# A cast behind a multiply, a scaling in two groups, keys ahead of values, and last columns of 384 and 128, in a fused attention and feed-forward kernel

## The chip, the cores and the metric

The kernel runs on one core of a Trainium2 chip. The metric is the device time of one execution in microseconds (us), as the median of several executions; lower is better. All executions quoted here were fast: TensorE's granted clock was 0.995 to 1.0 in them. Engine names are those of the profile: PE is TensorE, PEld its weight loads, DVE VectorE, ACT ScalarE, POOL GpSimd, SP SyncE; SPq and ACTq are the queues from which SP and ACT issue DMAs.

## The reference

Attention of a linear kind (8 batches, 8 heads, 576 positions, 64 wide) is followed by a gated feed-forward block, called FFN below.

```python
q_s = exp(q - max(q, -1));  q_s = q_s / (sum(q_s, -1) + 1e-9)     # over the 64 columns
k_s = exp(k - max(k, 2));   k_s = k_s / (sum(k_s, 2) + 1e-9)      # over the 576 positions
kv  = einsum('bhsd,bhse->bhde', k_s, v)
a   = einsum('bhsd,bhde->bhse', q_s, kv)                          # float32
x   = a.transpose(0, 2, 1, 3).reshape(4608, 512)
g   = x @ w_gate;  silu = g / (1 + exp(-g))                       # w_gate, w_val: 512 x 1536
out = (silu * (x @ w_val)) @ w_out                                # w_out: 1536 x 512, float32
```

## The kernel before

Heads are handled in two groups G of four heads. For a batch, ACT takes the exponentials of queries and keys, DVE normalises the queries (sum, reciprocal, multiply into `qs`), PE turns `qs`, multiplies keys with values (`kv`), DVE scales that by the key sums (`kn`), and PE multiplies the two into `xp`, which is copied into `xt`. The FFN then works through `xt` in chunks of tokens. A chunk has 12 units; unit m makes 128 of the 1536 hidden columns:

```python
def m_unit(c0, n, m, by_group=False):          # (cut)
    ...                                        # 4 matmuls g_ps <- xt,wg and 4 u_ps <- xt,wv
    nc.scalar.activation(out=sg, in_=g_ps, func=AF.Silu)
    nc.vector.tensor_mul(hr[:, m, ...], sg, u_ps)
```

PSUM is the memory that PE writes its results to. Every PSUM tile comes from one pool of eight banks, so a PE unit may have to wait until an earlier Silu has read its bank. Attention of later batches is woven between the units. Batch 1's is done between the first batch's FFN and the first chunk:

```python
def cast_v(b, G):                              # POOL: values to bf16
    return nc.gpsimd.tensor_copy(out=vbs[G][:, :, :, 0:64], in_=raw["v", b, G]...)

norm_sum(1, 0)
i = norm_mul(1, 0)
cast_v(1, 0)
c = cast_v(1, 1)                               # the second cast waits for the first multiply
tc.add_manual_dep(c.ins, i.ins.name, SYNC, reason="order of the vector port")
norm_sum(1, 1)
... # exponentials of the keys, turns of group 0, part of the output matmuls of block 2
norm_mul(1, 1)
... # turns of group 1
kv_both(1)                                     # K^T V of both groups in two banks
scale_both(1)                                  # two reciprocals and two multiplies on DVE
```

Loads are issued from SP in program order; `load_kv(b)` issues keys, values, keys, values. In the first chunk (batch 2) the exponentials of batch 3's keys stand ahead of the seventh unit:

```python
chunks = [(S, 448)] + [(c, 512) for c in range(1024, n_tok, 512)]
for ci, (c0, n) in enumerate(chunks):          # (cut: only what concerns chunk 0)
    for m in range(MT):
        if ci == 0 and m == 6:
            exp_of("k", b + 1, 0)              # ACT, needs batch 3's first keys
            exp_of("k", b + 1, 1)              # ACT, needs batch 3's second keys
            ...
        m_unit(c0, n, m)
```

The last 128 rows are made in two halves of columns, so that the first half is stored while the second is computed:

```python
def o_last(j):
    for c0 in (0, 256):
        o_ps = bank("o_ps")
        ...                                    # 12 matmuls of 256 columns
        nc.vector.tensor_copy(out=o_sb[:, c0:c0 + 256], in_=o_ps[:, 0:256])
        store(j, o_sb, c0, c0 + 256, (nc.sync, nc.scalar))   # 64 rows from each queue
```

The softmax here doesn't subtract the row's maximum and nothing guards it: scores larger than these inputs give would overflow.

## Time and profile before

| | before |
|---|---|
| time, first three runs | 314.22 us (313.61 to 314.38) |
| time, six runs, in the rounds of the result below | 313.74 us (313.46 to 314.38) |
| span in the profile | 311.3 us |
| PE busy | 301.7 us, 97% |
| first FFN matmul | 14.1 us |
| first FFN matmul of chunk 0 / of chunk 1 | 51.51 / 72.33 us |
| last matmul starts / last store lands | 306.49 / 310.12 us |

The head of the page of the kernel before gives the span, and for each engine busy time, share and number of instructions.

```profile
span 311.3 us, 5449 instructions
...
PE 301.7 (97%) x2182; PEld 149.7 (48%) x2182; DVE 161.3 (52%) x274; ACT 145.9 (47%) x214; POOL 31.2 (10%) x39
```

PE bounds the kernel. Whatever the change gains has to come from the ten microseconds in which PE is not busy, of which the head and the tail hold most. The view of waits of the kernel before, for PE (waited for, us in total, times, longest), lists two between 40 and 60 us:

```profile
PE tp L162 <- DVE qs L147: 0.6, 1, 0.6
...
PE g_ps L282 <- ACT sg L289: 0.3, 1, 0.3
```

The timeline of the kernel before shows what these are. Its columns are start, duration, engine, line, operation, tiles written and read, shapes, count, and in brackets the idle time ahead with its releaser.

```profile
44.31 1.15 POOL L122 CAST vb<-v 128x1152 bf16<-128x1152 f32 x1 [0.28 <-DVE rs L133]
44.62 2.04 DVE L147 TENSOR_TENSOR qs<-eq,rr 128x1152 bf16<-128x1152 bf16 x1
46.72 0.68 PE L162 MATMUL tp<-ident,qs 128*128 128x128 bf16 x9 [0.64 <-DVE qs L147]
...
54.91 1.16 ACT L119 ACTIVATE ek<-k 128x1152 bf16<-128x1152 f32 x1 [0.68 <-DMA k<-in_k_dram]
57.98 0.92 PE L282 MATMUL g_ps<-xt,wg 128*128 128x448 bf16 x4 [0.26 <-ACT sg L289]
...
64.66 1.16 ACT L119 ACTIVATE ek<-k 128x1152 bf16<-128x1152 f32 x1 [0.35 <-DMA k<-in_k_dram]
65.84 1.28 ACT L289 ACT_TABLE_LOAD   x1
67.90 0.92 PE L282 MATMUL g_ps<-xt,wg 128*128 128x448 bf16 x4
```

Three places matter. At 44.6 us the multiply for `qs` took 2.04 us while POOL cast values, and PE waited 0.64 us for it. At 54.9 us ACT had waited 0.68 us for batch 2's last keys; its first Silu came late and PE waited for a bank. At 64.7 us the same happened with batch 3's second keys, but there PE reached the unit concerned (unit 11, that is the eleventh, at 67.90 us) just as the bank came free, so PE lost nothing. This third place is called the gate below.

The tail, by the timeline of the kernel before: the last copy.

```profile
306.80 0.42 DVE L331 COPY o_sb<-o_ps 128x256 f32<-128x256 f32 x1 [0.89 <-PE o_ps L327]
```

And by the DMA view of the kernel before, from 307.4 us to the end (packets, MB and share of the 16 DMA engines' time in the window; then each issue with KB and us from issue to landing):

```profile
q14 instruction: 2, 0.02, 2.4%
...
out_dram<-o_sb SPq DMA_DIRECT2D x1, 64.0 KB, 2.7
out_dram<-o_sb ACTq DMA_DIRECT2D x1, 64.0 KB, 2.9
```

The last two stores of 64 KB took 2.7 and 2.9 us to land.

### The profile page before, as it was taken

What the parts mean: (1) busy time and instruction counts of PE and PEld (TensorE: products, weight loads), DVE (VectorE), ACT (ScalarE), POOL (GpSimd) and SP (SyncE); (2) the same over time, 40 slices, a digit from 0 to 9 for tenths busy, and PEclk for the clock granted to TensorE, in tenths of its full rate; (3) what the DMA queues carried; (4) which work ended last, traced back from release to release, by engine and by line L of the source; (5) the groups of instructions that cost most, each with busy time, mean ns of one, the idle gap of its engine ahead of it and who ended that gap; (6) DMA issues with size and microseconds to landing.
All of it is one profiled execution on the core that took longest, in us unless ns stands there. A gap on an engine that the chain in (4) does not pass through costs nothing.

```text
span 311.3 us, 5449 instructions
## 1 busy us (share of the span) xinstructions
PE 301.7 (97%) x2182; PEld 149.7 (48%) x2182; DVE 161.3 (52%) x274; ACT 145.9 (47%) x214; POOL 31.2 (10%) x39
## 2 busy tenths in 40 slices
PE   6899999999999999999999999999999999999994
PEld 2578745555444444454445444544444444444443
DVE  3844487945853566365826493539353324333321
ACT  5843558785674375547464737454042113212200
POOL 2960031120200110002000200000000000000000
PEclk9999999999999999999999999999999999999998
DMA  7999999899346916490739252505310211021034
GB/s 274 190 198 204 278 388 390 283 258 392 81 86 180 345 28 119 117 393 17 143 71 375 81 124 61 180 0 106 73 34 2 67 24 44 2 68 25 9 71 101
DMA packets 41690, 45.78 MB, mean 147 GB/s; under 512 B 18496, under 2 KB 25664, under 8 KB 41664
## 3 DMA queue, kind: packets, MB, share of 16 engines
q1 hardware_dynamic: 32752, 39.99, 43.3%
q0 software_dynamic: 8752, 5.31, 11.9%
q8 instruction: 17, 0.28, 0.4%
q10 hardware_dynamic: 160, 0.13, 0.2%
q14 instruction: 9, 0.07, 0.1%
HBM read 37.75 MB, written 9.44 MB: 152 GB/s over the span
## 4 chain that ended last, share of the span: by engine, by line
PE 80%; DMA 12%; POOL 4%; ACT 1%; SPq 1%; issue 0%; DVE 0%; ACTq 0%
PE o_ps L307 26%; PE g_ps L282 26%; PE u_ps L282 25%; DMA k<-in_k_dram 8%; DMA wo<-in_moe_w_out_dram 4%; POOL wg L94 1%; POOL wv L94 1%; PE kv L187 1%; PE xp L243 1%; PE o_ps L327 1%; ACT ek L119 1%; SPq L77 1%; POOL v L345 0%; ACT L289 0%; POOL v L342 0%
## 5 line engine op out<-in xcount | busy, mean ns | idle before, releaser
L289 ACT ACTIVATE sg<-g_ps 128x512 bf16<-128x512 f32 (+2 forms) x120 | 64.5, 554 | 133.0 <-PE g_ps L282 133.0
L290 DVE TENSOR_TENSOR hr<-sg,u_ps 128x512 bf16<-128x512 bf16 (+2 forms) x120 | 74.2, 630 | 87.9 <-PE u_ps L282 81.4
L282 PE MATMUL g_ps<-xt,wg 128*128 128x512 bf16 (+2 forms) x480 | 111.5, 358 | 0.3 <-ACT sg L289 0.3
L282 PE MATMUL u_ps<-xt,wv 128*128 128x512 bf16 (+2 forms) x480 | 111.4, 358 | 0.0
L307 PE MATMUL o_ps<-wo,hr 128*128 128x512 bf16 x420 | 93.9, 379 | 0.0
L282 PEld LDWEIGHTS <-wv 128*128 128x128 bf16 x480 | 46.9, 98 | 46.5
L282 PEld LDWEIGHTS <-wg 128*128 128x128 bf16 x480 | 46.2, 98 | 45.8 <-issue 0.7
L307 PEld LDWEIGHTS <-hr 128*128 128x128 bf16 x420 | 40.8, 98 | 48.6
L108 DVE COPY o_sb<-o_ps 128x512 f32<-128x512 f32 x33 | 22.4, 680 | 39.2 <-PE o_ps L307 39.2
L122 POOL CAST vb<-v 128x1152 bf16<-128x1152 f32 x14 | 16.3, 1162 | 137.2 <-DMA v<-in_v_dram 77.6
L133 DVE TENSOR_REDUCE rs<-eq 128x18 f32<-128x1152 bf16 (+2 forms) x18 | 21.7, 1214 | 12.8 <-ACT eq L119 12.8
L147 DVE TENSOR_TENSOR qs<-eq,rr 128x1152 bf16<-128x1152 bf16 (+2 forms) x18 | 22.4, 1254 | 0.1
L119 ACT ACTIVATE eq<-q 128x1152 bf16<-128x1152 f32 (+2 forms) x18 | 18.3, 1051 | 3.5 <-DMA q<-in_q_dram 3.5
L119 ACT ACTIVATE ek<-k 128x1152 bf16<-128x1152 f32 (+2 forms) x17 | 18.3, 1102 | 3.4 <-DMA k<-in_k_dram 3.3
L289 ACT ACT_TABLE_LOAD x12 | 15.4, 1283 | 0.2
L119 ACT ACT_TABLE_LOAD x11 | 14.1, 1283 | 0.2
L257 ACT CAST xt<-xp 128x512 bf16<-128x512 f32 x14 | 7.8, 586 | 4.1 <-PE xp L243 4.1
L258 DVE CAST xt<-xp 128x512 bf16<-128x512 f32 x14 | 9.0, 682 | 0.9 <-PE xp L243 0.9
L372 PE MATMUL idle<-zero 128*128 128x512 bf16 x20 | 6.5, 480 | 2.7 <-DVE rs L133 1.4
L187 PEld LDWEIGHTS <-ek 64*64 64x64 bf16 x504 | 6.4, 107 | 1.7 <-ACT ek L119 0.4
L187 PE MATMUL kv<-vb,ek 64*64 64x65 bf16 x504 | 6.8, 195 | 0.0
L243 PE MATMUL xp<-qt,kn 64*64 64x512 bf16 (+1 forms) x112 | 6.7, 292 | 0.0
(43 smaller groups left out, 63.2 us busy)
## 6 DMA issues: line engine op xcount, KB each, us to landing
q<-in_q_dram SPq DMA_DIRECT2D x16, 576.0 KB, 5.6
out_dram<-o_sb SPq DMA_DIRECT2D x70, 128.0 KB, 2.3
k<-in_k_dram SPq DMA_DIRECT2D x15, 576.0 KB, 7.9
v<-in_v_dram SPq DMA_DIRECT2D x14, 576.0 KB, 9.5
wo<-in_moe_w_out_dram POOLq DMA_DIRECT2D x4, 384.0 KB, 14.4
wg<-in_moe_w_gate_dram POOLq DMA_DIRECT2D x2, 384.0 KB, 10.1
wv<-in_moe_w_val_dram POOLq DMA_DIRECT2D x2, 384.0 KB, 11.4
wg<-in_moe_w_gate_dram POOLq DMA_DIRECT2D x2, 256.0 KB, 6.4
```

Source lines behind the costliest of these rows:

```text
L108: eng.tensor_copy(out=out, in_=in_)
L119: nc.scalar.activation(out=e[:, t0:t1], in_=src[:, t0:t1], func=AF.Exp)
L122: return nc.gpsimd.tensor_copy(out=vbs[G][:, :, :, 0:64], in_=raw["v", b, G].rearrange("p h (t d) -> p t h d", d=64),)
L133: i = nc.vector.reduce_sum(out=rs[:, 2 * t0:2 * t1], in_=eq2[:, 2 * t0:2 * t1, :], axis=mybir.AxisListType.X)
L147: last = eng.tensor_mul(qs[:, t0:t1, :].rearrange("p t (h d) -> p (t h) d", d=64), eq2[:, 2 * t0:2 * t1, :], s["rr"][:, 2 * t0:2 * t1].to_ ...
L187: nc.tensor.matmul(out=kv[g][HALF[h], c:c + 65], lhsT=ek[HALF[g], t, h, :], rhs=vbs[G][HALF[g], t, h, :], start=(t == 0), stop=(t == T - 1),)
L243: nc.tensor.matmul(out=o[h][HALF[g], c:c + 64 * (t1 - t0)], lhsT=kn[HALF[h], g, G, :], rhs=qt[G][HALF[h], t0:t1, 64 * g:64 * g + 64], star ...
L258: nc.vector.tensor_copy(out=xt[:, 2 * G + 1, c0:c0 + 512], in_=main[G][1])
L282: nc.tensor.matmul(out=gu[a][i][:, 0:w_], lhsT=(wg, wv)[a][:, kk, ms], rhs=xt[:, kk, c:c + w_], start=(kk == 0), stop=(kk == KT - 1),)
L289: nc.scalar.activation(out=sg[:, 0:w_], in_=g_ps[:, 0:w_], func=AF.Silu)
L290: nc.vector.tensor_mul(hr[:, m, r:r + w_], sg[:, 0:w_], u_ps[:, 0:w_])
L307: nc.tensor.matmul(out=o_ps, lhsT=hr[:, m, r0:r0 + 128], rhs=wo[:, m, :], start=(m == 0), stop=(m == MT - 1),)
```

## The change

The intent was to keep POOL off the vector port while the second query multiply runs, to hand K^T V of batch 1 on group by group, to have batch 2's keys loaded ahead of its values since ACT needs them first, to spread copies of the head over engines and banks, and to leave less to copy and store after the last matmul.

```diff
-        for c0 in (0, 256):
+        for c0, n in ((0, 384), (384, 128)):         # o_last; 256 becomes n in its body
...
         turn_pe(0, 1, 0)                              # head
+        turn_out(0, 1, 0, nc.vector)
+        xp0 = x_mm(0, 0, 0), x_mm(0, 0, 1)
         turn_pe(0, 1, 1)
-        turn_out(0, 1, 0, nc.vector)
         turn_out(0, 1, 1, nc.vector)
-        xp0 = x_mm(0, 0, 0), x_mm(0, 0, 1)
         kv_first(1, *BANKS[0])
         kv_first(1, *BANKS[1])
-        x_out(0, 0, 0, xp0[0])
+        x_out(0, 0, 0, xp0[0], (nc.scalar, None))
         x_out(0, 0, 1, xp0[1], (nc.scalar, None))
         scale_first(1, nc.vector)
+        x_out(0, 0, 0, xp0[0], (None, nc.scalar))
         x_out(0, 0, 1, xp0[1], (None, nc.vector))
...
-        load("q", q, 2, 0)                            # loads of batch 2
-        load("q", q, 2, 1)
-        load_kv(2)
+        for what, src in (("q", q), ("k", k), ("v", v)):
+            for G in range(NG):
+                load(what, src, 2, G)
...
-        i = norm_mul(1, 0)                            # batch 1
-        cast_v(1, 0)
-        c = cast_v(1, 1)
-        tc.add_manual_dep(c.ins, i.ins.name, SYNC, reason="order of the vector port")
+        norm_mul(1, 0)
...
-        norm_mul(1, 1)
+        i = norm_mul(1, 1)
+        cast_v(1, 0)
+        c = cast_v(1, 1)
+        tc.add_manual_dep(c.ins, i.ins.name, SYNC, reason="order of the vector port")
...
-        st["kv", 1] = [bank("kv") for _ in range(2)]
+        kv = [[bank("kv") for _ in range(2)] for _ in range(NG)]
-        kv_both(1)
-        scale_both(1)
+        kn = st["kn", 1] = at.tile([128, 2, NG, 64], BF16, tag="kn2", name="kn2")
+        for G in range(NG):
+            kv_mm(1, G, kv[G], 0)
+            for g in range(2):
+                kvr = at.tile([128, 1], FP32, tag=f"kvr{g}", name="kvr")
+                nc.vector.reciprocal(out=kvr, in_=kv[G][g][:, 64:65])
+                nc.vector.tensor_scalar_mul(kn[:, g, G], kv[G][g][:, 0:64], kvr)
```

Cut away: pieces of output matmuls are moved to fill PE (4 and 10 become 6 and 9), and `exp_of("k", 1, 0)` stands four operations later. In the built programs, DVE has 455 instructions instead of 452 (the scaling by group adds four, one copy goes to ACT).

More of the change, by code (lines that the diff above doesn't have):

```diff
@@ L217, in kv_both @@
     def kv_both(b):
-        if ("kv", b) not in st:
-            st["kv", b] = [bank("kv") for _ in range(2)]
+        kv = st["kv", b] = [bank("kv") for _ in range(2)]
         for G in range(NG):
-            kv_mm(b, G, st["kv", b], 256 * G)
+            kv_mm(b, G, kv, 256 * G)
     def scale_both(b):
@@ L327, in o_last @@
                 nc.tensor.matmul(
-                    out=o_ps[:, 0:256], lhsT=hr[:, m, r0:r0 + 128], rhs=wo[:, m, c0:c0 + 256],
+                    out=o_ps[:, 0:n], lhsT=hr[:, m, r0:r0 + 128], rhs=wo[:, m, c0:c0 + n],
                     start=(m == 0), stop=(m == MT - 1),
                 )
-            nc.vector.tensor_copy(out=o_sb[:, c0:c0 + 256], in_=o_ps[:, 0:256])
-            store(j, o_sb, c0, c0 + 256, (nc.sync, nc.scalar))
+            nc.vector.tensor_copy(out=o_sb[:, c0:c0 + n], in_=o_ps[:, 0:n])
+            store(j, o_sb, c0, c0 + n, (nc.sync, nc.scalar))
     make_identity(nc, ident)
@@ L460 @@
         o_out(1, o_mm(1), nc.scalar)
-        exp_of("k", 1, 0)
         p2 = o_mm(2, m1=4)
@@ L465 @@
         turn_out(1, 0, 0, nc.scalar)
+        exp_of("k", 1, 0)
         exp_of("k", 1, 1, BANKS)
-        norm_mul(1, 1)
+        i = norm_mul(1, 1)
+        cast_v(1, 0)
+        c = cast_v(1, 1)
+        tc.add_manual_dep(c.ins, i.ins.name, SYNC, reason="order of the vector port")
         o_mm(2, p2, m0=4)
@@ L473 @@
         turn_out(1, 1, 1, nc.vector)
-        st["kv", 1] = [bank("kv") for _ in range(2)]
-        p3 = o_mm(3, m1=4)
+        kv = [[bank("kv") for _ in range(2)] for _ in range(NG)]
+        p3 = o_mm(3, m1=6)
         o_out(2, p2)
-        kv_both(1)
-        scale_both(1)
+        kn = st["kn", 1] = at.tile([128, 2, NG, 64], BF16, tag="kn2", name="kn2")
[5 more added lines that the diff above has]
+                nc.vector.tensor_scalar_mul(kn[:, g, G], kv[G][g][:, 0:64], kvr)
         exp_of("q", 2, 0)
-        o_mm(3, p3, m0=4, m1=10)
+        o_mm(3, p3, m0=6, m1=9)
         x_and_next_kv(1, with_kv=False)
-        o_mm(3, p3, m0=10)
+        o_mm(3, p3, m0=9)
         o_out(3, p3)
```

## The prediction

> **What bounds the kernel.** The page gives PE 301.7 of 311.3 us busy (97%), and the waits of PE sum to under 5 us. Besides the head (14.1 us to the first FFN matmul) the timeline leaves:
> - 46.1 to 46.7 us: PE waits for batch 1's second normalised query group (0.64 us). That DVE multiply took 2.04 us, its twin 1.36, while the POOL value cast (44.31, 1.15 us) ran. The Trainium skill, "SBUF — State Buffer", section "SBUF: two separate sides", calls the port pair shared by Vector and GpSimd an exclusive lock held for a whole instruction; 0.68 us lost against 0.84 us of overlap agrees roughly.
> - 57.55 to 57.98 us: PE waits for a PSUM bank that the first Silu of batch 2's first chunk (57.39 us) frees, late because ACT waited 0.68 us for batch 2's last keys (they landed at 54.83) and then loaded a table (1.28 us).
> - The tail: last matmul 306.8, copy 0.42 us, last store issued 307.26, landed 310.1.
>
> **What the change does.**
> 1. Cast moved behind the multiply: it ends near 45.98, so PE resumes near 46.05: 0.65 us.
> 2. K^T V scaled by group: eight short DVE operations (start to start about 0.2 us) instead of four. They start near 48.4 and end near 50.1; PE's second group of attention matmuls waits for that: about 0.3 us given back. The first FFN matmul of the next chunk comes near 51.1 instead of 51.51: 0.4 us.
> 3. Keys ahead of values: loads land one after another, 1.5 us apart, so the last keys land near 53.3. ACT no longer waits; the first Silu comes near 56.0; the gap at 57.6 (0.43 us) closes.
> 4. Head: same PE work, copies swap engines and hold two PSUM banks longer: -0.1 to +0.1 us.
> 5. Tail: the last copy shrinks from 0.42 to about 0.28 us (estimate: 0.69 us at 512 columns, 0.42 at 256), and the last store halves. But the first copy grows to 0.55, and both queues still issue the 384-column stores when the second copy ends. Gain 0 to 0.2 us. (128-column matmuls at 56 ns, as the transposes ran.)
>
> **How much stays.** Locally 0.8 us is gained by 58 us. Most should be lost at the next gate: batch 3's second key group lands at 64.64 (its issue follows the same loads and stores, so it will not move). Then exp 1.16, table 1.28, and the seventh Silu runs 67.14 to 67.68. The eleventh FFN unit needs the PSUM bank that this Silu frees. Before, PE got there at 67.90, just after; now it gets there at 67.1 and waits until about 67.73. The DVE multiplies behind it (67.71 to 70.46) then hold batch 2's attention matmuls (69.5 to 70.8) too. So 0.8 shrinks to 0.1 to 0.2 us. From 71 us PE runs without waits to the end.
>
> Sum: -0.1 to -0.2 in the middle, -0.1 at the tail. 314.2 becomes 314.0 us; range 313.3 to 314.6; faster by over 2% 0.01, within 2% 0.98, slower 0.01.
>
> **What would show it.** The multiply at 1.36 us; no PE wait for qs at 46; batch 2's last keys at 53.3; no PE wait for Silu at 57.6; a new PE wait on Silu of about 0.6 us near 67.1; the eleventh unit starting 67.7 to 67.8; seventh Silu still at 67.1; last store issued near 307.1.
>
> **What would make it wrong.** Batch 3's keys landing earlier (then up to 0.9 us is gained); the cast or the eight-step scaling delaying PE by more than the slack of 0.65 us; a bank wait in the head that outlives the weights' arrival; two simultaneous stores at the tail interfering.

## The result, and the profile after

The changed kernel ran in 313.08 us (median of 6, 312.61 to 313.54), the kernel before in the same rounds in 313.74 us (median of 6). The ratio is 0.9975, with a 95% interval of 0.9959 to 0.9991. Ratios here are the mean time of one kernel's fast runs over that of the other's fast runs of the same rounds, so not quite the ratio of the medians quoted. The outcome is "same" at 2%, as predicted, but 313.08 lies below the predicted range of 313.3 to 314.6.

Two later repetitions belong to the result, in the first and the fourth call below: 0.9984 (0.9967 to 1.0002) and 1.0007 (0.9986 to 1.0027).

The head of the page of the kernel after, and two lines from its view of PE's waits:

```profile
span 311.2 us, 5454 instructions
...
PE 303.4 (98%) x2182; PEld 150.0 (48%) x2182; DVE 161.0 (52%) x277; ACT 146.7 (47%) x215; POOL 31.8 (10%) x39
```

```profile
PE g_ps L281 <- ACT sg L288: 0.8, 1, 0.8
PE xp L200 <- DVE kn L407: 0.4, 1, 0.4
```

The wait for `qs` is gone and the one for a Silu has grown. (The second line is a wait in the head, at 13.9 us; the kernel before had one of 0.6 us there, for ACT.) The timeline of the kernel after, at the three places:

```profile
44.78 1.36 DVE L147 TENSOR_TENSOR qs<-eq,rr 128x1152 bf16<-128x1152 bf16 x1
46.20 0.68 PE L162 MATMUL tp<-ident,qs 128*128 128x128 bf16 x9
46.20 1.15 POOL L122 CAST vb<-v 128x1152 bf16<-128x1152 f32 x1 [2.02 <-DVE qs L147]
...
52.50 2.22 ACT L119 ACTIVATE ek<-k 128x1152 bf16<-128x1152 f32 x2
57.46 0.92 PE L281 MATMUL g_ps<-xt,wg 128*128 128x448 bf16 x4
...
65.25 1.16 ACT L119 ACTIVATE ek<-k 128x1152 bf16<-128x1152 f32 x1 [1.45 <-DMA k<-in_k_dram]
66.43 1.28 ACT L288 ACT_TABLE_LOAD   x1
68.32 0.92 PE L281 MATMUL g_ps<-xt,wg 128*128 128x448 bf16 x4 [0.77 <-ACT sg L288]
```

The multiply takes 1.36 us and PE no longer waits for it. ACT takes both key exponentials of batch 2 without a wait, and PE does not wait at 57.5 us. But at the gate ACT waits 1.45 us for batch 3's second keys, and unit 11 starts at 68.32 us, 0.42 us later than before. Chunk 1 starts at 72.82 us instead of 72.33, although the head was only 0.16 us later. From there to the last matmul, both kernels take the same time within 0.06 us (234.16 and 234.22 us).

The tail of the kernel after, by the timeline and then by the DMA view from 307.9 us:

```profile
306.63 0.96 DVE L330 COPY o_sb<-o_ps 128x384 f32<-128x384 f32 x2 [1.26 <-PE o_ps L326]
```

```profile
q14 instruction: 1, 0.01, 1.3%
...
out_dram<-o_sb SPq DMA_DIRECT2D x1, 32.0 KB, 2.0
out_dram<-o_sb ACTq DMA_DIRECT2D x1, 32.0 KB, 2.2
```

From the start of the last matmul (307.04 us) to the last landing (310.02 us) it takes 2.98 us instead of 3.62. So the tail gives 0.64 us, and the middle takes about half of it back in this profile (0.49 less the 0.16 of the head, so 0.33 us). Both differ from the prediction (0 to 0.2 us gained at the tail, 0.1 to 0.2 us gained in the middle).

Two theories were needed. For the tail: the smaller last store (theory S, called T when it was first tested) or something that only comes with the change. For the middle: the gate (theory G), where a gain ahead of batch 3's keys turns into a wait for them, or theory M, that the gain of the middle is carried to the end.

### The profile page after: what moved, and what is told of

Its sections match the earlier page's. It is cut to its first block, busy times and chain, and to the rows that moved or that the text cites. A ratio compares the mean times of both kernels' runs of the same rounds, so it can differ in the third digit from the quotient of the medians.

```text
span 311.2 us, 5454 instructions
## 1 busy us (share of the span) xinstructions
PE 303.4 (98%) x2182; PEld 150.0 (48%) x2182; DVE 161.0 (52%) x277; ACT 146.7 (47%) x215; POOL 31.8 (10%) x39
## 4 chain that ended last, share of the span: by engine, by line
PE 91%; DMA 4%; ACT 3%; issue 1%; DVE 0%; ACTq 0%
PE o_ps L306 29%; PE g_ps L281 28%; PE u_ps L281 28%; DMA k<-in_k_dram 2%; PE xp L242 2%; PE kv L187 1%; PE idle L371 1%; DMA q<-in_q_dram 1%; PE o_ps L326 1%; ACT L288 1%; ACT sg L288 1%; PE tp L162 1%; ACT ek L119 1%; PE xp L200 0%; ACT eq L119 0%
## 5 line engine op out<-in xcount | busy, mean ns | idle before, releaser
L147 DVE TENSOR_TENSOR qs<-eq,rr 128x1152 bf16<-128x1152 bf16 (+2 forms) x18 | 21.7, 1216 | 0.1
L371 PE MATMUL idle<-zero 128*128 128x512 bf16 x20 | 7.8, 555 | 2.6 <-DVE rs L133 1.4
```

The costliest lines, as they stand in the source:

```text
L147: last = eng.tensor_mul(qs[:, t0:t1, :].rearrange("p t (h d) -> p (t h) d", d=64), eq2[:, 2 * t0:2 * t1, :], s["rr"][:, 2 * t0:2 * t1].to_ ...
L371: i = nc.tensor.matmul(out=idle, lhsT=zero[:, 0:128], rhs=zero, start=True, stop=True)
```

## The experiments

18 runs were made, some of them repeats of a kernel, on five chips in turn, each call with its own runs of the kernel before. "Tail" is the time from the start of the last matmul to the last landing in the profile. "Landing" is that of batch 3's second keys.

### First call: repeat, tail alone, and the gate opened in both (before 313.58 us)

The changed kernel unchanged:

> The changed kernel once more. Theory G (gate): batch 3's last keys land at a time that varies from run to run (64.64 us in the first profile of before, 65.22 in that of after), and the time follows it, so the runs of this kernel spread by up to 0.9 us and have a mean 0.5 to 0.9 us below before. PE's wait for the seventh Silu is there again in the profile, and ends 2.5 us after that landing (exp, table load, Silu). Theory M (the middle's 0.8 us is carried to the end): the mean is about 0.8 us below and the wait at 67 us is an accident of one profile, so absent here.

It ran in 313.24 us, 0.9984 (0.9967 to 1.0002). Tail 3.08 us. The keys landed at 64.89 us; PE, whose head was 1 us late in this profile, reached unit 11 later than the bank and did not wait.

The kernel before with only the last columns changed:

```diff
-        for c0 in (0, 256):
+        for c0, n in ((0, 384), (384, 128)):
```

> Before with the last output columns split 384 and 128 instead of 256 and 256, nothing else. The profile of after suggests that the tail from the last full output tile's end to the end of the span is 0.5 us shorter, against 0 to 0.2 predicted. Theory T (tail): this alone gives 0.4 to 0.6 us, ratio 0.998 to 0.9987, most of the measured gain. Theory M: at most 0.2 us, ratio 0.9994 or more.

It ran in 314.09 us, 1.0011 (0.9996 to 1.0026), and its tail was 3.92 us, longer than the kernel before's 3.62. The smaller last store alone gains nothing here, against theory S. (A clean test had to wait for the third call, since a fetch fell among the last stores of this kernel too.)

The changed kernel with batch 3's keys ahead of its values, which should open the gate:

```diff
-        load_kv(3)
+        for what, src in (("k", k), ("v", v)):
+            for G in range(NG):
+                load(what, src, 3, G)
```

> After with batch 3's loads in the order keys, keys, values, values too. Its second key group should land one load (1.5 us) earlier, near 63.5 us. Theory G: PE's wait for the seventh Silu vanishes and the kernel runs 0.6 to 1.2 us faster than after, 1.2 to 1.8 us faster than before. Theory M or T alone: within 0.2 us of after.

It ran in 312.58 us, 0.9971 (0.9955 to 0.9986). The keys landed at 63.31 us. The timeline of this kernel at the gate:

```profile
62.56 2.22 ACT L119 ACTIVATE ek<-k 128x1152 bf16<-128x1152 f32 x2
64.79 1.28 ACT L288 ACT_TABLE_LOAD   x1
...
67.31 0.92 PE L281 MATMUL g_ps<-xt,wg 128*128 128x448 bf16 x4
```

ACT takes both exponentials without a wait and unit 11 starts at 67.31 us, without a wait. The mean is 0.5 us below that of the repeat above, less than the 0.6 to 1.2 us expected.

The same edit in the kernel before:

> Before with batch 3's keys ahead of its values, nothing else. In the profile of before PE reached the gate 0.2 us after the Silu was done, so the gate costs nothing there when the keys land at 64.64. Theory G: 0 to 0.3 us faster than before (only the runs with late keys gain). If it gains as much as the same edit on after, theory G is wrong in saying that the other parts of the change feed the gate.

It ran in 313.51 us, 0.9999 (0.9983 to 1.0015): opening a gate that holds nothing gains nothing. Its tail was 3.80 us. So of the difference between the last two kernels, 0.7 us is tail (3.10 against 3.80), with the last columns not yet excluded as a partner of something else in the change.

### Second call: what shortens the tail (before 313.78 us)

The DMA packet records of the trace around the last stores show packets of kind `instruction`: 16 KB on queue 8, 17 in a run, and 8 KB on queue 14. One 8 KB packet began at 308.41 us in the kernel before, 1.9 us after the last matmul started and in the middle of the last stores, but at 305.91 us in the kernel after, 1.1 us ahead of that matmul. In both it came when 447 DVE instructions had been recorded, and earlier ones came at 193 and 319 (before) and 189 and 315 (after), so every 126 to 132 DVE instructions, which suggests that it fetches DVE's program. (Queue 14 carries other 8 KB packets, at other counts.) The new theory F: three more DVE instructions anywhere ahead bring this fetch forward, out of the way of the last stores; the split of the columns does not matter.

The changed kernel with 256 and 256 columns again:

```diff
-        for c0, n in ((0, 384), (384, 128)):
+        for c0, n in ((0, 256), (256, 256)):
```

> After with the last output columns 256 and 256 again. So far the tail from PE's last matmul start to the last landing took 3.63 us in before, 2.98 and 3.08 in after, but 3.92 when only the split was made. Theory F (fetch): in before two 8 KB instruction fetches run among the last stores (308.4 and 309.0 us); in after one of them ran 2.5 us earlier, because VectorE's program is three instructions longer there, all from the group-wise scaling and the moved copy. So without the split the tail stays short: 3.0 to 3.3 us, an instruction fetch is 2 to 3 us ahead of the tail, and the time is within 0.3 us of after. Theory S (split): 3.6 to 3.9 us, 0.6 us slower than after.

It ran in 313.22 us, 0.9981 (0.9958 to 1.0004). Tail 3.03 us: short without the changed columns. Here the gate cost PE 0.90 us (landing 65.48, unit 11 at 68.57 us).

The kernel before with nothing but three tiny DVE instructions early in the program, whose result nobody uses:

```diff
+        pad = const.tile([128, 3], FP32, name="pad", tag="pad")
+        for i in range(3):
+            nc.vector.memset(pad[:, i:i + 1], 0.0)
```

> Before with three memsets of one column each added to VectorE's program near the start, where it waits for data anyway. No other change. Theory F: the fetch that was at 308.4 us moves 2 to 3 us earlier, the tail shrinks from 3.63 to 3.0 to 3.3 us, and the kernel is 0.3 to 0.6 us faster than before. Theory S: tail 3.6 to 3.8 us, same time.

It ran in 312.76 us, 0.9968 (0.9948 to 0.9989), and its tail was 3.06 us. The DMA view of this kernel from 307.4 us on:

```profile
q14 instruction: 1, 0.01, 1.1%
...
out_dram<-o_sb SPq DMA_DIRECT2D x1, 64.0 KB, 1.9
out_dram<-o_sb ACTq DMA_DIRECT2D x1, 64.0 KB, 2.3
```

One instruction packet instead of two, and stores of the same 64 KB that land after 1.9 and 2.3 us instead of 2.7 and 2.9. Three instructions that only add work took about as much time off as the whole change.

The changed kernel with the scaling of both groups together again (451 DVE instructions, one fewer than before):

```diff
-            kv_mm(1, G, kv[G], 0)                     # and four DVE operations for each group
+            kv_mm(1, G, st["kv", 1], 256 * G)
+        scale_both(1)
```

> After with the K^T V of batch 1 scaled by both groups together again (four VectorE operations instead of eight). Theory F: VectorE's program is one instruction shorter than that of before, so the fetch is back in the tail, which takes 3.6 to 4.0 us although only the middle was edited; 0.6 us or more slower than after. Theory S: tail 3.0 us as in after. In the middle: the attention matmuls start later (about 50.0 us) and the next chunk's first FFN matmul is within 0.2 us of after's 51.4.

It ran in 313.17 us, 0.9989 (0.9964 to 1.0014). Tail 3.06 us, with the fetch 4.75 us after the start of the last matmul, when the stores had landed. Theory F had expected a long tail here, and missed: the fetch can be out of the way on either side. The landing was 64.26 us and the gate did not hold.

Keys first for batch 3 only, batch 2 as before:

```diff
-        for what, src in (("q", q), ("k", k), ("v", v)):   # batch 2
-            for G in range(NG):
-                load(what, src, 2, G)
+        load("q", q, 2, 0)
+        load("q", q, 2, 1)
+        load_kv(2)
-        load_kv(3)                                         # batch 3: k, k, v, v
```

> After with batch 3's keys first (as in e3), and batch 2's loads in the order of before. Theory G: with the gate open, each part's local gain shows in the end. Batch 2's last keys land 1.5 us later, PE waits 0.4 to 0.9 us for the first Silu of the chunk near 57.5 us, and from the first o_ps matmul to the next chunk's first FFN matmul it takes 34.4 to 34.9 us against 34.0 in e3; 0.4 to 0.8 us slower than e3.

It ran in 312.89 us, 0.9969 (0.9947 to 0.9991), tail 3.09 us, no wait at the gate. It does not separate from the third kernel of the first call (312.58 us), so the worth of batch 2's order of loads was not resolved.

### Third call: the count of 452 hit on purpose, and the gate made worse (before 313.78 us)

These rounds were noisier than the others (standard deviation 0.6 to 1.0 us).

The kernel with 451 DVE instructions, one memset added, so 452 again:

```diff
+        pad = const.tile([128, 1], FP32, name="pad", tag="pad")
+        for i in range(1):
+            nc.vector.memset(pad[:, i:i + 1], 0.0)
```

> The kernel of e7 with one memset of one column added at the start of VectorE's program, so that it has as many VectorE instructions as before (452), while after has 455 and e7 451. In e7 the fetch fell after the tail (4.75 us past PE's last matmul start) and the tail was short. Theory F: with 452 the fetch is back among the last stores, 1.9 to 2.4 us past that matmul, the tail is 3.6 to 4.0 us and the kernel 0.5 to 0.9 us slower than e7. Theory S: 3.0 us, same time as e7.

It ran in 314.88 us, 1.0024 (0.9995 to 1.0054). Tail 3.99 us. The DMA view of this kernel from 308.7 us on:

```profile
q14 instruction: 2, 0.02, 1.6%
...
out_dram<-o_sb SPq DMA_DIRECT2D x1, 32.0 KB, 3.1
out_dram<-o_sb ACTq DMA_DIRECT2D x1, 32.0 KB, 3.2
```

One more memset than the kernel with 451, and the tail is 0.93 us longer; stores of 32 KB took over 3 us. Between the two profiles the last landing is 2.27 us later: 0.93 us is the tail, and 1.47 us is a head that was late in this profile (first FFN matmul at 15.83 instead of 14.36 us).

Both the split and the three memsets in the kernel before:

> e2 and e6 together: before with the 384 and 128 split and the three memsets. Theory F: tail 2.9 to 3.1 us, as in after and e6, 0.8 us shorter than e2; the time is that of e6 within 0.3 us, 0.5 to 1.0 us below before. Theory S (the split has its own effect, only hidden in e2): 0.3 us or more below e6.

It ran in 313.40 us, 0.9977 (0.9950 to 1.0004). Tail 3.03 us, no shorter than with 256 columns and the memsets (3.06).

The changed kernel with batch 3's keys last:

```diff
-        load_kv(3)
+        for what, src in (("v", v), ("k", k)):
+            for G in range(NG):
+                load(what, src, 3, G)
```

> After with batch 3's values ahead of its keys, so that the second key group lands one load (1.5 to 2 us) later than in after, near 66.5 to 67.3 us. Theory G: the eleventh FFN unit of that chunk starts 3.1 us after that landing, as in after and e5 (3.09 and 3.10), near 69.6 to 70.4, PE waits 2 us or more there, and the kernel is 1.2 to 2.0 us slower than after. Theory M: within 0.3 us of after.

It ran in 315.27 us, 1.0036 (1.0013 to 1.0060). The keys landed at 67.94 us, later than expected. PE at the gate, from the timeline of this kernel:

```profile
71.03 0.92 PE L281 MATMUL g_ps<-xt,wg 128*128 128x448 bf16 x4 [2.62 <-ACT sg L288]
```

Unit 11 starts 3.09 us after the landing, and within 0.01 us so it does in the kernel after (65.22 to 68.32), in the one with the tail undone (65.48 to 68.57) and in the third repeat below (65.95 to 69.04). That fixed distance shows the gate: when the keys are late enough, PE waits for them through the Silu.

Keys first, and four more ACT instructions at the end, to see if the other instruction packet (2.5 to 2.8 us after the start of the last matmul in every profile) is ACT's:

```diff
+        pad = const.tile([128, 4], FP32, name="pad", tag="pad")
+        for i in range(4):
+            nc.scalar.activation(out=pad[:, i:i + 1], in_=warm, func=AF.Silu)
```

> e3 (after with batch 3's keys first) with four one-column activations added to ScalarE's program after the last Silu, where it is idle. The other 8 KB fetch, at 2.5 us past PE's last matmul start in every profile so far, belongs to ScalarE if it moves: theory F then has it some 10 us earlier and the tail at 2.7 to 3.0 us instead of 3.10, 0 to 0.3 us faster than e3. If it doesn't move, it is another engine's.

It ran in 313.00 us, 0.9963 (0.9939 to 0.9988), tail 3.05 us. The packet stayed at 2.52 us. It is not ACT's; whose it is stays open.

### Fourth call: the three memsets against the change, gate closed and open (before 313.57 us)

The four kernels are the kernel before with three memsets, the changed kernel, and each of the two with batch 3's keys first. Edits as above.

> e6 again, as the base of the two by two. Tail 3.0 to 3.1 us; 0.4 to 0.8 us faster than before.

> After, with the same tail as e13. Theory G: the gate takes back what the middle gains, so the mean is within 0.25 us of e13, and where the head was on time the profile shows PE waiting at the eleventh unit until 3.1 us after the landing of batch 3's last keys. Theory M: 0.6 us or more faster than e13.

> e13 with batch 3's keys first. Theory G: 0 to 0.25 us faster than e13, as PE's own waits at 46 and 57 us come first there.

> e3 again. Theory G: the fastest of the four, 0.3 to 0.9 us faster than e14 and than e15; no PE wait for Silu after 45 us. If it is within 0.2 us of e15, the middle gains nothing even with the gate open.

| kernel | median, mean (us) | ratio to before | tail | landing | unit 11 |
|---|---|---|---|---|---|
| before and three memsets | 313.00, 312.95 | 0.9975 (0.9963 to 0.9987) | 3.03 | 64.49 | 68.10 |
| changed | 313.81, 313.94 | 1.0007 (0.9986 to 1.0027) | 2.94 | 65.95 | 69.04, after a wait of 1.16 |
| before, memsets, keys first | 313.23, 313.09 | 0.9980 (0.9968 to 0.9991) | 3.07 | 64.22 | 68.46 |
| changed, keys first | 313.05, 313.26 | 0.9987 (0.9970 to 1.0004) | 3.02 | 63.42 | 67.99 |

With equally short tails, the changed kernel is 1.0 us slower than three memsets while the gate is closed (one of its six runs, 315.56 us, makes up part of that mean; by medians it is 0.8 us). That misses the expected 0.25 us. Of the 0.99 us between the last landings of the two profiles, 0.72 us is a later head (first FFN matmul at 14.51 against 13.79 us) and 0.30 us the stretch from there to chunk 1, so most of it is not the gate.

Opening the gate made the changed kernel faster by 0.7 us here and by 0.5 us in the first call (means, with intervals that overlap). It did nothing for the old middle (0.9999 in the first call, 0.1 us slower here). But with the gate open, the changed kernel and three memsets differ by 0.2 us only, slower by the means and faster by the medians. The expectation had named this beforehand as the sign that the middle gains nothing even with the gate open. So it is shown that the gate costs the changed kernel time (PE waited 0.77 to 1.16 us there in three of its four profiles, that with the tail undone counted in), but not that there was a gain of 0.8 us in the middle to be taken.

### Fifth call: is PE's own instruction fetch what delays the keys? (before 313.61 us)

In the profiles of the changed kernel and of it with the columns undone, the load of the second keys itself took long: it landed 1.94, 1.83, 2.54 and 2.74 us after the load ahead of it, against 1.48 to 1.87 us in the kernel before and its variants (and 1.49 us in the changed kernel with the scaling undone). A 16 KB instruction packet falls near that time (63.06 us in the kernel after, 63.97 us before). To move it, 14 matmuls of 2 columns were added in the head to the kernel with three memsets; the second kernel is that one without them.

```diff
-        spin(8)
+        spin(8, tiny=14)                  # 14 matmuls of 2 columns ahead of the first 8 warm-up matmuls
```

> e6 with 14 matmuls of two columns added to PE's program at the very start, in a time in which PE waits for data, so that each later fetch of PE's program comes 28 instructions (about 1.3 us) earlier. Theory P (PE's fetch delays the load in whose time it falls): the 16 KB fetch at 64.3 to 64.7 us in e6 and e13 moves to 62.7 to 63.4, batch 3's last keys then land 1.9 us or more after the load ahead, and the eleventh FFN unit of the chunk waits for Silu; 0.3 to 0.9 us slower than e18. Rival C (the later landing is chance, or another part of the middle's): the load takes 1.5 to 1.9 us as in e6 and e13, no wait for Silu at the eleventh unit, same time as e18.

> e6 and e13 once more, as the base of e17. 0.4 to 0.9 us faster than before; tail 3.0 to 3.1 us; batch 3's last keys 1.5 to 1.9 us after the load ahead.

They ran in 312.63 us, 0.9970 (0.9957 to 0.9984), and 312.97 us, 0.9979 (0.9965 to 0.9994). The fetch moved by 1.3 us early in the program, but stood at 63.69 us in the stretch in question. The manipulation failed, so the experiment says nothing about its theory. The kept traces say more. As worded, theory P does not hold: in the kernel before, in it with the columns changed and with three memsets (last repeat), the fetch began while the keys were loading, 0.89, 1.10 and 1.14 us after the load ahead had landed, and the keys took 1.55, 1.48 and 1.53 us. But over the 13 profiles with `load_kv(3)`, the three long key loads (1.94, 2.54 and 2.74 us) are just those in which the fetch began early, from 0.23 us before to 0.65 us after that landing; in the other ten it began 0.8 us or more after it. This was seen afterwards, and no run succeeded in moving the fetch there on purpose, so it is a lead and not a shown cause. Why the keys land later in the changed kernel stays open. The second kernel is a third confirmation of the memsets.

### The tails together

| kernel | DVE instructions | last columns | DVE's fetch, us from the last matmul's start | tail, us |
|---|---|---|---|---|
| before | 452 | 256, 256 | +1.91 | 3.62 |
| before, keys first | 452 | 256, 256 | +1.92 | 3.80 |
| before, columns changed | 452 | 384, 128 | +2.39 | 3.92 |
| scaling undone, one memset | 452 | 384, 128 | +2.43 | 3.99 |
| scaling undone | 451 | 384, 128 | +4.75 | 3.06 |
| changed | 455 | 384, 128 | -1.13 | 2.98 |
| changed, columns undone | 455 | 256, 256 | -1.08 | 3.03 |
| before, three memsets | 455 | 256, 256 | -0.83 | 3.06 |
| before, memsets, columns changed | 455 | 384, 128 | -1.13 | 3.03 |

The tail goes with the count and not with the columns. The packet records also show how. Each last store is 80 packets, so five for each of 16 DMA engines. In the kernel before, all packets of the last ACT-queue store but five had ended by 309.10 us, and the last five ended from 309.31 to 309.46; on the SP queue the same, 308.83 and then 309.06 to 309.20. In the kernel with 451 instructions and one memset (452) the break is 310.29, then 310.71 to 310.93. With 455 instructions there is no break: after, the last ones end at 309.53, 309.54, 309.54, 309.57 and 309.57 us. That five is one engine's share, and that this engine was busy with the 8 KB packet (308.41 to 309.02 us in the kernel before), is argued: the records do not name the engine.

## Why the prediction was wrong

"Within 2%" was right, the time was not: 313.08 us against 314.0 predicted. Of these 0.9 us, 0.5 is the kernel before itself, which ran in 313.74 us in the rounds of the result and in 314.22 us in the three runs that the prediction started from. The rest is a change of 0.66 us (by medians) instead of 0.2. That is itself one draw: by means, the three measurements of the change gave 0.8 and 0.5 us faster and 0.2 us slower. Point by point:

1. "Cast moved behind the multiply ... 0.65 us." The mechanism held: the multiply took 1.36 us and the wait was gone. The Trainium skill, "SBUF — State Buffer", section "SBUF: two separate sides", says that the port pair shared by DVE and POOL is an exclusive lock for the whole instruction. The runs agree well: the multiply loses the overlap with the cast less 0.15 to 0.16 us each time (overlap 0.84, loss 0.68 in the kernel before; 1.03 and 0.87 in it with keys first; 0.50 and 0.35 with three memsets). The size was one draw of several, though. In the kernel before and its variants PE's wait was 0.6, 0.2, 0.8 and, in five of the six profiles with three memsets, 0.3 us. The second cast starts 0.13 us after its values land or, in those six, as soon as the first cast ends. And the change leaves the first cast free: in three profiles of the changed kernel and its variants that one began ahead of the first multiply, which then took 1.66, 1.66 and 2.04 us instead of 1.36, and PE waited 0.2, 0.3 and 0.6 us there. For the overlap of 0.50 us, here are the two casts and the second multiply of the kernel before with three memsets, last repeat, from its timeline; the two casts end at 45.19 us:

```profile
41.90 3.29 POOL L122 CAST vb<-v 128x1152 bf16<-128x1152 f32 x2 [19.13 <-DMA v<-in_v_dram]
...
44.69 1.71 DVE L147 TENSOR_TENSOR qs<-eq,rr 128x1152 bf16<-128x1152 bf16 x1
```

2. "About 0.3 us given back" by scaling in groups: in the profile chunk 0 started 0.10 us earlier than before (51.41 against 51.51) with a head 0.16 us later. Predicted was 0.4 us earlier. Undoing the scaling alone gave 313.17 us on one chip, but with a different tail fetch and a different landing; its own worth was not resolved.
3. "The last keys land near 53.3 ... the gap at 57.6 closes": keys at 53.24 us, first Silu at 56.03 us (predicted 56.0), no wait. Right, though the idle time that closed was 0.26 us by the profile, not 0.43.
4. Head "-0.1 to +0.1 us": from the first K^T V matmuls of the head to the first FFN matmul, it took 3.26 us in the first changed profile and 3.20 us before, and in the median 3.06 us over the eleven profiles with the changed head and 3.21 us over the nine with the old one. About right. The first FFN matmul itself came at 14.43 and 14.06 us in the median; whether the change has a part in that was not tested.
5. "Gain 0 to 0.2 us" at the tail: this is the step that failed: the term of the sum was mis-sized, and for a wrong reason. It measured 0.64 us. The copy did shrink from 0.42 to 0.29 us, but the last store was issued 0.83 us after the start of the last matmul, against 0.77 us before, so the smaller last piece gained nothing on the issue. The gain is in the landing, and it comes from three DVE instructions added elsewhere by the scaling, which moved an instruction fetch out of the stores. Neither the prediction nor the change had this in view.
6. "Most should be lost at the next gate": the mechanism is right, and is shown by the fixed 3.09 us from landing to unit 11 in four profiles. "It will not move" is the second step that failed: in the first pair the landing came 0.59 us later, PE waited 0.77 us at the gate, and the middle lost 0.33 us instead of gaining 0.1 to 0.2. Over all profiles, the keys landed at 65.22, 64.89, 65.48 and 65.95 us in the four profiles of the changed kernel and of it with the tail undone, against 63.28 to 64.91 us in the seven profiles of the kernel before and its variants with `load_kv(3)`. From the first output matmul to unit 11, those four took 30.56 us in the mean (29.98 to 31.00), those seven 30.01 us (29.50 to 30.58). With keys first the changed kernel took 30.00 us in the mean of three profiles, so 0.56 us less, but no less than those seven: the local gain of 0.8 us that the prediction counted on is not seen there either. Two of these three profiles had a wait elsewhere (0.56 us for `qs`, 0.46 us for output weights). The cause of the later landing is the open point of the fifth call.

Summed over the first pair of profiles: tail 0.64 us gained, middle 0.33 us lost, head 0.16 us lost, 0.06 us lost between chunk 1 and the last matmul; that leaves about 0.1 us, as the last landings say (310.02 against 310.12 us). The difference to the 0.66 us of the timed medians is within what the arrival of the head's first loads does from run to run: the first FFN matmul came anywhere from 13.62 to 15.83 us over the profiles. The safest statement on the change is the three ratios together, 0.9975, 0.9984 and 1.0007, beside 0.9968, 0.9975 and 0.9979 for the kernel before with three memsets. No version beat that one clearly; the changed kernel with keys first (0.9971 and 0.9987; with batch 2's order of loads undone 0.9969, with four more ACT instructions 0.9963) and the one with 14 tiny matmuls (0.9970) are as fast within the intervals.

## What to carry to other kernels

Before crediting a change of the tail, look in the DMA view for instruction packets among the last stores, and repeat the old kernel with a few idle instructions added: if that gains as much, the change's own work was not the cause. A gain ahead of a wait for a load counts only up to that wait, so find that landing first, bring it forward together with the change, and check that the gain then shows in the time; here it did not clearly. When a gap depends on the moment at which a load lands, cost it from several profiles, not from one.

## What the Trainium skill lacked or had wrong

- "Runtime: NRT & Kernel Launch", section "Instruction fetch mechanics", says that the sequencer fetches the next page by its own DMA queue while the current one runs, in blocks of 16 KiB or 256 instructions, and that the cost of crossing a block's boundary is mostly hidden. The trace agrees with 16 KB for one group of packets (17 on queue 8), but DVE's come in packets of 8 KB, every 126 to 132 instructions, and in the tail one cost time all the same: tails of 3.62 to 3.99 us with it among the last stores, 2.94 to 3.10 us without.
- "DMA: Bandwidth & Descriptors", section "Issuing engines are not separate DMA queues", says that DMAs of all issuing engines interleave on the same 16 DMA engines. It does not speak of instruction packets. The two of 8 KB among the last stores of the kernel before took 0.61 and 0.53 us, and five packets of each last store ended 0.2 to 0.4 us behind the other 75; that they share a DMA engine is argued above, not recorded.
- "TensorE: Matmul & The Clock Gate", section "Back-to-back issue gap", gives about 81 ns for each matmul of 128 columns in a stream with weight loads. The 12 of the changed kernel's end, each with its own weights, started 56 ns apart (306.43 to 307.04 us), which is what the page gives for an isolated one.
